# A scheduled attention and expert kernel: elementwise work moved from GpSimd to VectorE, new planner rules, a third buffer

## The chip, the cores and the metric

The kernel runs on one core of a Trainium2 chip. The metric is the device time of one execution in microseconds (us). The kernel before took 844.2 us, the median of 3 runs (843.67 to 844.75).

## The reference

Three stages follow one another, in float32 (2 batches, 8 heads, 576 positions, head size 64; so 1152 tokens of 512):

```python
# 1 attention, with the 32 largest scores of each row kept
scores = scale * np.matmul(q, k.transpose(0, 1, 3, 2))
kth = np.partition(scores, -32, axis=-1)[..., -32:-31]
attn = softmax(np.where(scores >= kth, scores, -1e9))   # written out
x = (attn @ v), heads side by side                      # 1152 x 512
# 2 four experts, all of them for every token
for e in range(4):                                      # w1[e] 512 x 1024, w2[e] 1024 x 512
    y += p[:, e:e+1] * (np.maximum(x @ w1[e], 0.0) @ w2[e])
# 3 a gated layer                                       # w_a, w_b 512 x 1536, w_out 1536 x 512
return (y @ w_a) * (y @ w_b) @ w_out
```

The three weights of stage 3 come in as 64-bit floats, and the kernel makes float32 of them itself.

## The kernel before

**Work.** The 1152 tokens are nine tiles of 128, in four groups of 1, 2, 3 and 3 tiles. While one group is in the top-32 search of stage 1 (VectorE, L772 and L780), TensorE works on the experts of the groups before it. Matrices are multiplied in a reduced float format, so each operand is split into a high part (a copy on ScalarE) and a low part (operand minus high part), and a product is three matmuls (high x high, high x low, low x high). L492 is the line of every matmul, L495 that of every transpose.

Per expert and group: ScalarE evicts relu(x w1) as the high part (L1007), VectorE makes the low part (L1011); both free the PSUM bank and feed the second matmul. L1036 adds the results to y. The weights' own parts are L937 (ScalarE) and L938 (GpSimd for the early groups, VectorE for the late ones).

Stage 3 computes y w_a and y w_b together by Strassen's scheme, with seven products of half size in place of eight. It needs sums of y's parts first. `combine` makes them, once for group 2 (with all groups before it) and once for group 3 (`own`). For each half: four `whole` sums of a high and a low part (L1085), the differences s1, s3, s2, s4 (L1108 to L1111; s1 of group 3 is L1105), a high part (L1112) and its low part (L1113), and three of each at once (L1115, L1116). In group 2 all but the high parts run on GpSimd. In group 3 the differences run on VectorE and the four sums on GpSimd; L1095 to L1103 evict the transposed y. `multiply` then evicts a first product with ScalarE (L1328), adds the other six to it on VectorE (L1319), multiplies the two results on GpSimd (L1322, twice), and splits the outcome into a high part (L1339, ScalarE) and a low part (L1340, GpSimd). There are 24 such calls: six steps, two units each, two sets of columns (320 and 256 wide). The second matmul adds up over the steps in SBUF (L1361, L1364).

The weights of stage 3 are prepared in the background: `double` makes a float32 from a 64-bit one with three VectorE instructions (the first L1224, the last L1227), two on ScalarE and an integer addition on GpSimd (L1230); `narrow` and `d_unit` make sums and parts of these (L1246, L1247, L1266 to L1273).

**Buffers.** The intermediate sums of `combine` and `multiply` lie in slots named tp, of which there are two, in the region `low`. A slot is free when its last reader is done.

**Order.** Nothing of this is ordered by hand. Each call registers an `Op` with its engine, a cost, a key (a smaller one goes first), what it waits for and the slots it uses. `Plan.order` simulates all engines, and at each step gives a free engine the ready Op of the smallest key. It does so 42 times with random delays added; from the seventh time on the early part is kept from the best order so far, up to one of the times in `STAGES` (50 to 400 us). `rerun` then goes through each order three times with delays, and the one with the smallest mean end is emitted. Each engine's instructions run in that order on the chip and wait for semaphores only. An Op with `port=True` (VectorE instructions that work in SBUF alone) isn't started in the simulation while GpSimd is busy:

```python
ok = not (op.port and free.get("POOL", 0.0) > now)
```

Of the kernel before, what the change touches and what calls it, by code (L numbers as in the profile page):

```python
# [84 lines left out]
class Op:  # L85
    __slots__ = ("engine", "hold", "lag", "key", "emit", "waits", "after", "tiles", "n", "start", "left", "at", "nbytes", "port", "late", "since")

SEEN, SEEN_PE = 45, 130  # L90
COLD, COLD_END = 1.7, 46e3
ISSUE, LAND, GBS, LANES = 500, 2100, 320.0, 8

STAGES = 0.0, 50e3, 110e3, 170e3, 230e3, 300e3, 400e3
ORDERS, RERUNS, SHAKE, LATE_ENGINE, LATE_DMA, LOG = 42, 3, 25.0, 40.0, 800.0, False


class Plan:  # L100
# [37 lines left out]
    def rerun(self, got, draw):  # L138

        free, end, dma, users = {}, {}, 0.0, {}  # L140
        last = 0.0
        for op in got:
# [10 lines left out]
            if op.engine == "SP":  # L153
                free["SP"] = t + ISSUE
                dma = max(dma, t + ISSUE) + op.nbytes / GBS
                e = dma + LAND + draw.uniform(0.0, LATE_DMA)
            else:
                free[op.engine] = t + hold
                e = t + hold + op.lag + (draw.uniform(0.0, LATE_ENGINE) if op.engine != "PE" else 0.0)
# [8 lines left out]
    def order(self):  # L168
# [28 lines left out]
        dma_free, lanes = 0.0, []  # L197
        queue, now, done = [(op.since, -1, None) for op in self.ops if op.since], 0.0, []
        heapq.heapify(queue)
        seq = 0  # L200
# [25 lines left out]
        def pick(engine):  # L226
# [6 lines left out]
            while ready_:  # L233
                item = heapq.heappop(ready_)
                op = item[2]

                ok = not (op.port and free.get("POOL", 0.0) > now)
                for t in op.tiles:
                    if t.slot is None and (t.slots in stuck or place(t) is None):
                        if t.n == t.slots.next:  # L240
                            stuck.add(t.slots)
                        ok = False
                if ok:
                    found = op
# [8 lines left out]
        while len(done) < len(self.ops):  # L253
            moved = False
            for engine in free:
# [20 lines left out]
                else:  # L276
                    hold = op.hold * COLD if engine == "PE" and now < COLD_END else op.hold
                    free[engine] = now + hold
                    end = now + hold + op.lag + op.late
                heapq.heappush(queue, (end, op.n, op))  # L280
                heapq.heappush(queue, (free[engine], -1, None))
# [5 lines left out]
            while queue and queue[0][0] <= now:  # L287
# [3 lines left out]
                if isinstance(op, Buffer):  # L291
                    op.slots.free.add(op.slot)
                    continue
                for t in op.tiles:
# [18 lines left out]
def dve(n):  # L313
    return 62 + 1.04 * n
# [18 lines left out]
FILL = 9  # L333
SLACK = 1200

# [5 lines left out]
def body(tc, q, k, v, probs, w1, w2, wa, wb, wo, out):  # L341
# [61 lines left out]
    xf = const("xf", [128, KD, 128])  # L403
    vrem = [const(f"vrem{b}", [128, H, D]) for b in range(B)]
    qrem = const("qrem", [128, H, D])
    kscr = dr.tile([B, HP, 2 * D, 2, S], F32, name="kscr")
# [45 lines left out]
    vvs = low.slots("vv", 2, 2048)  # L452
    tps = low.slots("tp", 2, 4 * 320)
    mid.again()
# [597 lines left out]
    def combine(c, y, yd):  # L1052
# [9 lines left out]
        x0, x1 = slice(c0, c0 + n), slice(c1, c1 + n)  # L1062
        K = -1500 if own else -1000
        got = []
# [12 lines left out]
        def pair_(w, emit, after, tiles, sbuf=True):  # L1077
            if own:
                return vector(dve(w), lambda: emit(nc.vector), K, after, tiles, port=sbuf)
            return gpsimd(pool_(w), lambda: emit(nc.gpsimd), K, after, tiles)  # L1080

        def whole(out, k, cols, tp):
            w = cols.stop - cols.start
            return gpsimd(
                pool_(w), lambda: nc.gpsimd.tensor_tensor(out(), xs[:, 0, k, cols], xs[:, 1, k, cols], op=ALU.add), K,  # L1085
                sum((ydone[g, k] for g in range(len(GROUPS) - 1)), []), [tp]
            )
# [127 lines left out]
    def double(src, s, t, ts, n):  # L1215
# [14 lines left out]
        return gpsimd(pool_(512), lambda: nc.gpsimd.tensor_tensor(  # L1230
            t().bitcast(I32), fold(c.ap.bitcast(I32)), fold(lowv().bitcast(I32)), op=ALU.add), s, [o4, o5], [c, d, ts])

# [44 lines left out]
    def gated():  # L1277
# [32 lines left out]
        def multiply(un, own, g):  # L1310

            m = sets[own][2]
            tp = tps.tile()
            tv = lambda i, j=None: tp.ap[:, i * m:(j or i + 1) * m]
# [6 lines left out]
            def mul(out, i, j, after):  # L1321
# [103 lines left out]
```

## Time and profile before

| | |
|---|---|
| median of 3 runs | 844.2 us |
| profiled execution | 842.55 us, of it the span 840.8 us |
| TensorE busy | 800.8 us, 95% of the span |
| VectorE busy | 730.9 us, 87% |
| ScalarE busy | 535.1 us, 64% |
| GpSimd busy | 420.8 us, 50% |

All times come from one execution, and the shares are means over stages of different kinds. PE is TensorE, PEld its weight loads, DVE VectorE, ACT ScalarE, POOL GpSimd, SP the queue that issues transfers. L12 is line 12 of the kernel before. "Idle before" at an instruction or a group is the time in which its engine stood still just before it, with what ended that. Matmuls are pipelined, so their own durations overlap.

### The profile page before, as it was taken

The page shows a single profiled execution, that of the slowest core. Times are in us where ns is not written, and L with a number is a line of the kernel's source. Part 1 is how long each engine was busy: PE and PEld are TensorE (multiplying, and loading weights), DVE is VectorE, ACT ScalarE, POOL GpSimd, SP SyncE. Part 2 cuts the span into 40 slices and gives each one's busy share as a digit, 9 for nine tenths or more (in the row PEclk, how much of TensorE's full clock was granted, in tenths as well). Part 3 has the DMA queues.
Part 4 walks back from the last instruction along what each step waited for, and adds up shares of the span by engine and source line. Part 5 has one row for each costly group of instructions (what it writes and reads, how often), then busy time and mean ns, then how long its engine had stood idle before and what let it go on. Part 6 is the DMA issues. An engine that isn't in the chain of part 4 may idle for free.

```text
span 840.8 us, 14615 instructions
## 1 busy us (share of the span) xinstructions
PE 800.8 (95%) x5285; PEld 710.7 (85%) x5285; DVE 730.9 (87%) x1399; ACT 535.1 (64%) x953; POOL 420.8 (50%) x381
## 2 busy tenths in 40 slices
PE   7689999999999999999999998999999999999997
PEld 6577777798888889999899887888988889799996
DVE  7999999999899999999977967889858898986654
ACT  6879887998898989897756647666424532331210
POOL 3524433888977966854221393222226465372432
PEclk8699999999999999999999999999999999999999
DMA  6849977765455443523246637987311223211013
GB/s 218 249 132 318 326 214 215 228 182 180 154 189 155 132 151 102 169 76 126 76 128 195 190 114 274 318 281 249 104 50 51 101 79 100 73 51 50 2 51 112
DMA packets 91416, 129.68 MB, mean 154 GB/s; under 512 B 10832, under 2 KB 67152, under 8 KB 89808
## 3 DMA queue, kind: packets, MB, share of 16 engines
q1 hardware_dynamic: 91344, 128.75, 47.7%
q8 instruction: 41, 0.67, 0.3%
q14 instruction: 31, 0.25, 0.1%
HBM read 115.36 MB, written 13.37 MB: 153 GB/s over the span
## 4 chain that ended last, share of the span: by engine, by line
PE 52%; DVE 25%; ACT 8%; POOL 8%; issue 4%; DMA 2%; POOLq 0%; SPq 0%; DVEq 0%; ACTq 0%
PE ps L492 50%; DVE low L772 10%; DVE low L780 8%; PE ps L495 2%; POOL mid L938 2%; ACT low L803 1%; ACT mid L937 1%; POOL low L1085 1%; ACT low L811 1%; POOL low L1230 1%; DVE big L1273 1%; ACT lowa L751 1%; DVE low L1036 1%; POOL low L807 1%; DVE mid L1011 1%
## 5 line engine op out<-in xcount | busy, mean ns | idle before, releaser
L492 PE MATMUL ps<-mid 128*128 128x512 f32 x1092 | 279.5, 397 | 6.6 <-ACT mid L1007 3.2
L492 PEld LDWEIGHTS ps<-mid 128*128 128x128 f32 x1092 | 199.5, 189 | 45.0 <-ACT mid L1007 3.8
L492 PE MATMUL ps<-xs,mid 128*128 128x384 f32 (+1 forms) x1152 | 203.7, 321 | 3.5 <-DVE mid L1011 3.3
L492 PEld LDWEIGHTS ps<-xs,mid 128*128 128x128 f32 x1152 | 184.3, 189 | 13.1 <-DVE mid L1011 5.1
L772 DVE MAX8 low<-low 128x8 f32<-128x576 f32 x216 | 154.9, 747 | 0.1
L938 POOL TENSOR_TENSOR mid<-raw,mid 128x1024 fp32r<-128x1024 f32 x48 | 114.9, 2407 | 8.8 <-ACT mid L937 6.2
L807 POOL TENSOR_TENSOR low<-lowa,low 128x576 f32<-128x576 f32 x70 | 98.9, 1431 | 34.4 <-ACT low L803 28.1
L1230 POOL TENSOR_TENSOR low<-low 128x512 int32<-128x512 int32 x36 | 54.0, 1499 | 116.7 <-DVE low L1227 86.7
L937 ACT ACTIVATE mid<-raw 128x1024 fp32r<-128x1024 f32 x96 | 101.8, 1071 | 10.8 <-PE ps L492 9.4
L780 DVE MATCH_REPLACE8 low<-low 128x576 f32<-128x576 f32 x144 | 106.2, 743 | 0.0
L1319 DVE TENSOR_TENSOR low<-ps,low 128x320 f32<-128x320 f32 (+1 forms) x168 | 72.1, 452 | 27.0 <-PE ps L492 25.7
L1322 POOL TENSOR_TENSOR low<-low 128x320 f32<-128x320 f32 (+1 forms) x48 | 46.4, 968 | 91.6 <-DVE low L1319 82.0
L492 PE MATMUL ps<-xs,big 128*128 128x320 f32 (+1 forms) x576 | 87.5, 297 | 3.0 <-ACT low L1328 2.5
L492 PEld LDWEIGHTS ps<-xs,big 128*128 128x128 f32 x576 | 80.8, 190 | 6.2 <-ACT low L1328 2.8
L938 DVE TENSOR_TENSOR mid<-raw,mid 128x1024 fp32r<-128x1024 f32 x48 | 65.4, 1362 | 8.9 <-ACT mid L937 8.5
L1007 ACT ACTIVATE mid<-ps 128x384 fp32r<-128x384 f32 (+1 forms) x96 | 44.3, 465 | 38.2 <-PE ps L492 35.0
L492 PE MATMUL ps<-lowa_again,big 128*128 128x320 f32 (+1 forms) x432 | 66.9, 297 | 0.0
L1011 DVE SCALAR_TENSOR_TENSOR mid<-ps,mid 128x384 fp32r<-128x384 f32 (+1 forms) x96 | 47.9, 504 | 17.6 <-ACT mid L1007 17.4
L492 PEld LDWEIGHTS ps<-lowa_again,big 128*128 128x128 f32 x432 | 61.0, 190 | 2.4 <-DVE low L1319 0.6
L822 ACT ACTIVATE low<-low 128x576 f32<-128x576 f32 x70 | 51.5, 785 | 16.9 <-DVE low L819 16.8
L495 PE MATMUL ps<-identr,low 128*128 128x128 f32 x360 | 51.7, 279 | 9.8 <-ACT low L822 8.9
L803 ACT ACTIVATE low<-lowa,low 128x576 f32<-128x576 f32 x70 | 53.6, 782 | 11.6 <-POOL low L797 11.4
(119 smaller groups left out, 1240.7 us busy)
## 6 DMA issues: line engine op xcount, KB each, us to landing
raw<-in_moe_w_dram SPq DMA_DIRECT2D x122, 512.0 KB, 3.9
big<-kscr SPq DMA_DIRECT2D x20, 576.0 KB, 5.1
low<-in_v_dram SPq DMA_DIRECT2D x24, 256.0 KB, 3.5
low<-in_moe_w_b_dram SPq DMA_DIRECT2D x12, 512.0 KB, 3.6
low<-in_moe_w_a_dram SPq DMA_DIRECT2D x12, 512.0 KB, 4.3
low<-in_moe_w_out_dram SPq DMA_DIRECT2D x12, 512.0 KB, 4.2
wscr<-big SPq DMA_DIRECT2D x6, 1024.0 KB, 6.1
mid<-wscr SPq DMA_DIRECT2D x6, 1024.0 KB, 4.8
```

The lines of the kernel that those rows point to most:

```text
L492: nc.tensor.matmul(out, l, r, **kw)
L495: nc.tensor.transpose(out, a, i)
L772: 62 + 1.04 * width, lambda at=at, cs=cs: nc.vector.max(m8v()[:, x, cs], at()), key + 0.02 * r, [done],
L780: lambda at=at, cs=cs: nc.vector.match_replace(out=src[1](), in_to_replace=m8v()[:, x, cs], in_values=at(), imm_value=LOW),
L803: S, lambda x=x, s=s: nc.scalar.activation(ev(x), s.ap, AF.Relu, bias=endv()[:, x, 1:2], scale=-STEEP),
L807: pool_(S), lambda x=x, s=s: nc.gpsimd.tensor_tensor(ev(x), s.ap, ev(x), op=ALU.subtract), ks, [a], [s, ep]
L822: S, lambda x=x: nc.scalar.activation(ev(x), ev(x), AF.Copy, scale=sums.ap[:, x:x + 1]),
L937: hi = scalar(1024, lambda: nc.scalar.activation(u.ap[:, 0:1024], r.ap, AF.Copy), 500 + s, [ld], [u, r], sbuf=True)
L938: sub = lambda eng: eng.tensor_tensor(u.ap[:, 1024:2048], r.ap, u.ap[:, 0:1024], op=ALU.subtract)
L1011: lambda h=h, p=p: nc.vector.scalar_tensor_tensor(h.ap[:, n:2 * n], p.ap[:, 0:n], 0.0, h.ap[:, 0:n], op0=ALU.max, op1=ALU.subtract),
L1230: return gpsimd(pool_(512), lambda: nc.gpsimd.tensor_tensor(t().bitcast(I32), fold(c.ap.bitcast(I32)), fold(lowv().bitcast(I32)), op=ALU.a ...
L1319: return vector(dve(m), lambda: nc.vector.tensor_tensor(tv(out), p.ap[:, 0:m], tv(i), op=ALU.add), K, [o] + after, [p, tp])
```

## The change

Six things change. (1) The planner treats all GpSimd Ops as port Ops too, and starts neither engine's port Op while the other engine runs one. (2) Where two meet in a rerun, each goes on at a fixed share of its speed. (3) The sums and differences of `combine` for group 2 and the sums for group 3 go to VectorE, and those of group 2 get the key 1190 in place of -1000: behind all expert work (-100 and 500 on), just ahead of the weights of stage 3 (1210 on). (4) The low part in `multiply` (L1340) goes to VectorE. (5) A third tp slot lies in the memory of what is kept of v's and q's last rows, which attention reads; every third request takes it. (6) The planner reckons 600 ns more until the result of `double` is seen (`EASE`).

```diff
+OTHER = {"DVE": "POOL", "POOL": "DVE"}
+RATES = {"DVE": 0.65, "POOL": 0.5}
+def contend(engine, hold, other, left):
+    a, b = RATES[engine], RATES[other]
+    t = min(hold / a, left / b)
+    return t + hold - a * t, t + left - b * t
...
+BLOCK = True
@@ rerun, and the same in order, with the Op met pushed back to its later end
+                if op.port:
+                    other = OTHER[op.engine]
+                    y = runs.get(other)
+                    if y is not None and free[other] > t:
+                        hold, left = contend(op.engine, hold, other, free[other] - t)
+                        end[id(y)] += t + left - free[other]
+                        free[other] = t + left
@@ order, pick
-                ok = not (op.port and free.get("POOL", 0.0) > now)
+                y = runs.get(OTHER[engine]) if BLOCK and op.port else None
+                ok = y is None or free[y.engine] <= now
@@ body
-SLACK = 1200
+SLACK, EASE = 1200, 600
-    vrem = [const(f"vrem{b}", [128, H, D]) for b in range(B)]
-    qrem = const("qrem", [128, H, D])
+    rest = Region("rest", 3 * H * D, F32)
+    vrem = [rest.t[:, i * H * D:(i + 1) * H * D].rearrange("p (h d) -> p h d", d=D) for i in range(B + 1)]
+    qrem = vrem.pop()
-    tps = low.slots("tp", 2, 4 * 320)
+    tps = [low.slots("tp", 2, 4 * 320), rest.slots("tpr", 1, 4 * 320)]
+    def sums_slot():
+        taken_.append(0)
+        return tps[len(taken_) % 3 == 0].tile()
-    def gpsimd(hold, emit, key, after, tiles):
-        return plan.add("POOL", hold, emit, key, after, tiles, lag=55)
+    def gpsimd(hold, emit, key, after, tiles, lag=55):
+        return plan.add("POOL", hold, emit, key, after, tiles, lag=lag, port=True)
@@ combine
-        K = -1500 if own else -1000
+        K = -1500 if own else 1190
@@ pair_
-            if own:
-                return vector(dve(w), lambda: emit(nc.vector), K, after, tiles, port=sbuf)
-            return gpsimd(pool_(w), lambda: emit(nc.gpsimd), K, after, tiles)
+            return vector(dve(w), lambda: emit(nc.vector), K, after, tiles, port=sbuf)
@@ whole
-            return gpsimd(
-                pool_(w), lambda: nc.gpsimd.tensor_tensor(out(), xs[:, 0, k, cols], xs[:, 1, k, cols], op=ALU.add), K,
+            return vector(
+                dve(w), lambda: nc.vector.tensor_tensor(out(), xs[:, 0, k, cols], xs[:, 1, k, cols], op=ALU.add), K,
@@ half, multiply
-            tp = tps.tile()
+            tp = sums_slot()
@@ multiply
-            lo = gpsimd(pool_(2 * m), lambda: nc.gpsimd.tensor_tensor(
-                g.ap[:, n:2 * n][:, cs], tv(0, 2), g.ap[:, 0:n][:, cs], op=ALU.subtract), K, [hi], [g, tp])
+            lo = vector(dve(2 * m), lambda: nc.vector.tensor_tensor(
+                g.ap[:, n:2 * n][:, cs], tv(0, 2), g.ap[:, 0:n][:, cs], op=ALU.subtract), K, [hi], [g, tp], port=True)
```

What the new plan makes of it shows in the order of the instructions. The lines of the changed kernel have other numbers: L1126 there is L1085 here, L1149 to L1152 are L1108 to L1111, L1153, L1154, L1156 and L1157 are L1112, L1113, L1115 and L1116, L1050 and L1054 are L1007 and L1011, L980 and L981 are L937 and L938, L1137, L1144 and L1146 are L1096, L1103 and L1105, and L1369, L1360, L1363 and L1381 are L1328, L1319, L1322 and L1340.

GpSimd of the kernel before, where it makes the sums for group 2 (L1230 is the addition of `double`):

```order
L1230 TENSOR_TENSOR low<-low 128x512
L1085 TENSOR_TENSOR low<-xs 128x320 x4
L1108 TENSOR_TENSOR low<-low 128x320
L1109 TENSOR_TENSOR low<-low 128x320
L1113 TENSOR_TENSOR xs<-low,xs 128x320
L1110 TENSOR_TENSOR low<-low 128x320
L1111 TENSOR_TENSOR low<-low 128x320
L1116 TENSOR_TENSOR lowa_again<-low,lowa_again 128x3x320
L1085 TENSOR_TENSOR low<-xs 128x320 x4
```

The second half follows in the same way. In the changed kernel GpSimd has nothing at this place but the additions of `double`; the sums stand on VectorE, the first half as follows (L1265 to L1268 are `double`):

```order
L1126 TENSOR_TENSOR low<-xs 128x320 x3
L1054 SCALAR_TENSOR_TENSOR mid<-ps,mid 128x384 x2
L1126 TENSOR_TENSOR low<-xs 128x320
L1265 TENSOR_SCALAR low<-low 128x512
L981 TENSOR_TENSOR mid<-raw,mid 128x1024
L1149 TENSOR_TENSOR low<-low 128x320
L1266 TENSOR_SCALAR low<-low 128x512
L1150 TENSOR_TENSOR low<-low 128x320
L1154 TENSOR_TENSOR xs<-low,xs 128x320
L1151 TENSOR_TENSOR low<-low 128x320
L1268 SCALAR_TENSOR_TENSOR low<-low 128x512
L1152 TENSOR_TENSOR low<-low 128x320
```

So they are spread among expert work and weights. ScalarE at the same place, before:

```order
L1007 ACTIVATE mid<-ps 128x384
L1112 ACTIVATE xs<-low 128x320
L1007 ACTIVATE mid<-ps 128x384
L937 ACTIVATE mid<-raw 128x1024
L1115 ACTIVATE lowa_again<-low 128x3x320
L1007 ACTIVATE mid<-ps 128x384
```

and ScalarE in the changed kernel:

```order
L1153 ACTIVATE xs<-low 128x320
L1050 ACTIVATE mid<-ps 128x384
L980 ACTIVATE mid<-raw 128x1024
L1050 ACTIVATE mid<-ps 128x384
L1156 ACTIVATE lowa_again<-low 128x3x320
L1050 ACTIVATE mid<-ps 128x384
```

The copy that waits for the last difference (L1115, now L1156) stands one eviction of an expert later. On VectorE that difference follows that eviction's low part in the changed kernel:

```order
L1151 TENSOR_TENSOR low<-low 128x320
L981 TENSOR_TENSOR mid<-raw,mid 128x1024
L1054 SCALAR_TENSOR_TENSOR mid<-ps,mid 128x384
L1152 TENSOR_TENSOR low<-low 128x320
L1266 TENSOR_SCALAR low<-low 128x512
```

So the second difference of the pair now waits for an expert's eviction between the two. VectorE where the sums for group 3 are made, before:

```order
L1096 TENSOR_TENSOR xs<-ps,xs 128x128
L1105 TENSOR_TENSOR low<-ps,low 128x256
L1103 TENSOR_TENSOR xs<-ps,xs 128x384
L1109 TENSOR_TENSOR low<-low 128x256
L1110 TENSOR_TENSOR low<-low 128x256
L1113 TENSOR_TENSOR xs<-low,xs 128x256
L1111 TENSOR_TENSOR low<-low 128x256
L1105 TENSOR_TENSOR low<-ps,low 128x256
L1109 TENSOR_TENSOR low<-low 128x256
L1110 TENSOR_TENSOR low<-low 128x256
L1116 TENSOR_TENSOR lowa_again<-low,lowa_again 128x3x256
```

and in the changed kernel, from the same instruction to the first L1157 (L1381 is the low part of a product, in the slot of the new region `rest`):

```order
L1137 TENSOR_TENSOR xs<-ps,xs 128x128
L1152 TENSOR_TENSOR low<-low 128x256
L1126 TENSOR_TENSOR low<-xs 128x128
L1144 TENSOR_TENSOR xs<-ps,xs 128x384
L1146 TENSOR_TENSOR low<-ps,low 128x256
L1381 TENSOR_TENSOR mid<-rest,mid 128x640
L1157 TENSOR_TENSOR lowa_again<-low,lowa_again 128x3x256
L1150 TENSOR_TENSOR low<-low 128x256
L1154 TENSOR_TENSOR xs<-low,xs 128x256
L1151 TENSOR_TENSOR low<-low 128x256
L1360 TENSOR_TENSOR rest<-ps,rest 128x320
```

Ahead of these rows stand L1137, L1146, L1126, L1144, L1150, L1154 and L1151, each once, behind the seven additions of the product before. The low part now stands on VectorE, ahead of L1157, and the additions of the next product follow. Two of the four sums of group 3 (L1126, 128 columns) are made long before, behind those of group 2; the other two stand here.

## Rows read from the trace of the kernel before

**Rows 1.** Busy time by stage: stretch, length, PE, PEld, DVE, ACT, POOL, clock, DMA, GB/s.
```profile
302.00:480.00 178.00, 177.58 (x1236) 161.94 (x1235) 165.09 (x312) 138.10 (x249) 74.88 (x67) 1.00 0.40 128
480.00:520.00 40.00, 36.35 (x172) 31.53 (x171) 26.29 (x31) 20.63 (x33) 29.90 (x24) 0.96 0.55 172
520.00:600.00 80.00, 78.49 (x393) 70.30 (x392) 71.59 (x104) 50.06 (x76) 21.29 (x14) 1.00 0.80 267
600.00:632.00 32.00, 29.84 (x176) 27.86 (x174) 21.37 (x39) 10.71 (x24) 5.79 (x8) 1.00 0.17 53
632.00:756.00 124.00, 121.21 (x765) 110.25 (x766) 107.00 (x198) 49.13 (x79) 72.67 (x58) 1.00 0.24 77
756.00:836.00 80.00, 80.00 (x491) 73.40 (x489) 46.55 (x85) 11.09 (x19) 26.63 (x26) 1.00 0.14 49
836.00:841.00 5.00, 0.03 (x1) 0.00 (x0) 0.69 (x1) 0.00 (x0) 0.00 (x0) 0.81 0.43 127
```
**Rows 2.** TensorE's waits from 302 us on: for whom, us in total, times, longest.
```profile
PE ps L492 <- ACT mid L1007: 3.2, 2, 2.5
PE ps L492 <- ACT low L1328: 2.5, 1, 2.5
PE ps L492 <- DVE mid L1011: 2.0, 2, 1.5
PE ps L492 <- DVE raw L1364: 1.4, 3, 0.5
```
**Rows 3.** The chain that ended last, 478 to 510 us: start, us, what.
```profile
480.80 4.33 POOL low L1085 x4
...
494.45 5.23 POOL low L1085 x4
```
**Rows 4.** Instructions in order of time near 506 us: start, us, what [idle before].
```profile
505.52 1.00 ACT L1115 ACTIVATE lowa_again<-low 128x960 fp32r<-128x960 f32 x1 [3.07 <-POOL low L1111]
...
506.96 5.43 PE L492 MATMUL ps<-mid 128*128 128x512 f32 x15 [2.54 <-ACT mid L1007]
```
**Rows 5.** The same view, 623 to 633 us.
```profile
623.91 0.29 DVE L1096 TENSOR_TENSOR xs<-ps,xs 128x128 fp32r<-128x128 f32 x1
...
626.47 1.66 POOL L1340 TENSOR_TENSOR mid<-low,mid 128x640 fp32r<-128x640 f32 x1 [0.84 <-ACT mid L1339]
626.72 1.68 DVE L1110 TENSOR_TENSOR low<-low 128x256 f32<-128x256 f32 x1
...
631.89 0.44 ACT L1328 ACTIVATE low<-ps 128x320 f32<-128x320 f32 x1 [1.10 <-DVE lowa_again L1116]
...
632.38 1.15 PE L492 MATMUL ps<-xs,big 128*128 128x320 f32 x6 [2.54 <-ACT low L1328]
```
**Rows 6.** The same view, 584 to 590 us.
```profile
584.72 2.06 POOL L1230 TENSOR_TENSOR low<-low 128x512 int32<-128x512 int32 x1 [9.86 <-DVE low L1227]
585.55 1.52 DVE L1224 TENSOR_SCALAR low<-low 128x512 f32<-128x512 f32 x1
...
588.78 1.49 PE L492 MATMUL ps<-xs,mid 128*128 128x384 f32 x7 [1.51 <-DVE mid L1011]
```
**Rows 7.** GpSimd by shape, 302 us on: count, busy us, mean ns, idle before.
```profile
L1340 POOL TENSOR_TENSOR mid<-low,mid 128x640 fp32r<-128x640 f32 x12 | 19.0, 1587 | 10.7 <-ACT mid L1339 10.7
L1340 POOL TENSOR_TENSOR mid<-low,mid 128x512 fp32r<-128x512 f32 x12 | 16.7, 1389 | 9.7 <-ACT mid L1339 9.7
```
**Rows 8.** VectorE in the same view.
```profile
L1247 DVE TENSOR_TENSOR big<-low,big 128x512 fp32r<-128x512 f32 x12 | 9.3, 779 | 3.8 <-ACT big L1246 3.8
...
L1116 DVE TENSOR_TENSOR lowa_again<-low,lowa_again 128x768 fp32r<-128x768 f32 x2 | 1.9, 948 | 0.0
...
L1109 DVE TENSOR_TENSOR low<-low 128x256 f32<-128x256 f32 x2 | 0.8, 420 | 0.1
...
L1096 DVE TENSOR_TENSOR xs<-ps,xs 128x128 fp32r<-128x128 f32 x2 | 0.6, 286 | 0.1
```
**Rows 9.** GpSimd's busy time on L1340 alone in one stretch: us (count), clock, DMA.
```profile
632.00:756.00 124.00, 21.09 (x14) 1.00 0.24 77
```

More of the change, by code (lines that the diff above doesn't have):

```diff
@@ L85 @@
 class Op:
-    __slots__ = ("engine", "hold", "lag", "key", "emit", "waits", "after", "tiles", "n", "start", "left", "at", "nbytes", "port", "late", "since")
+    __slots__ = ("engine", "hold", "lag", "key", "emit", "waits", "after", "tiles", "n", "start", "left", "at", "nbytes", "port", "late", "since", "fin")
 SEEN, SEEN_PE = 45, 130
 COLD, COLD_END = 1.7, 46e3
+OTHER = {"DVE": "POOL", "POOL": "DVE"}
[4 more added lines that the diff above has]
+    return t + hold - a * t, t + left - b * t
 ISSUE, LAND, GBS, LANES = 500, 2100, 320.0, 8
 STAGES = 0.0, 50e3, 110e3, 170e3, 230e3, 300e3, 400e3
+BLOCK = True
 ORDERS, RERUNS, SHAKE, LATE_ENGINE, LATE_DMA, LOG = 42, 3, 25.0, 40.0, 800.0, False
@@ L140, in rerun @@
         free, end, dma, users = {}, {}, 0.0, {}
-        last = 0.0
+        last, runs = 0.0, {}
         for op in got:
@@ L157, in rerun @@
             else:
+                if op.port:
[5 more added lines that the diff above has]
+                        free[other] = t + left
+                if op.engine in OTHER:
+                    runs[op.engine] = op if op.port else None
                 free[op.engine] = t + hold
@@ L198, in order @@
         queue, now, done = [(op.since, -1, None) for op in self.ops if op.since], 0.0, []
+        runs = {}
         heapq.heapify(queue)
@@ L277, in order @@
                     hold = op.hold * COLD if engine == "PE" and now < COLD_END else op.hold
+                    if op.port:
+                        other = OTHER[engine]
+                        y = runs.get(other)
+                        if y is not None and free[other] > now:
+                            hold, left = contend(engine, hold, other, free[other] - now)
+                            y.fin += now + left - free[other]
+                            free[other] = now + left
+                            heapq.heappush(queue, (y.fin, y.n, y))
+                            heapq.heappush(queue, (free[other], -1, None))
+                    if engine in OTHER:
+                        runs[engine] = op if op.port else None
                     free[engine] = now + hold
                     end = now + hold + op.lag + op.late
+                op.fin = end
                 heapq.heappush(queue, (end, op.n, op))
@@ L292, in order @@
                     op.slots.free.add(op.slot)
+                    continue
+                if op.fin > now:
                     continue
@@ L452, in body @@
     vvs = low.slots("vv", 2, 2048)
-    tps = low.slots("tp", 2, 4 * 320)
+    tps = [low.slots("tp", 2, 4 * 320), rest.slots("tpr", 1, 4 * 320)]
+    taken_ = []
+    def sums_slot():
+        taken_.append(0)
+        return tps[len(taken_) % 3 == 0].tile()
     mid.again()
@@ L1077, in pair_ @@
         def pair_(w, emit, after, tiles, sbuf=True):
-            if own:
-                return vector(dve(w), lambda: emit(nc.vector), K, after, tiles, port=sbuf)
-            return gpsimd(pool_(w), lambda: emit(nc.gpsimd), K, after, tiles)
+            return vector(dve(w), lambda: emit(nc.vector), K, after, tiles, port=sbuf)
         def whole(out, k, cols, tp):
             w = cols.stop - cols.start
-            return gpsimd(
-                pool_(w), lambda: nc.gpsimd.tensor_tensor(out(), xs[:, 0, k, cols], xs[:, 1, k, cols], op=ALU.add), K,
-                sum((ydone[g, k] for g in range(len(GROUPS) - 1)), []), [tp]
+            return vector(
+                dve(w), lambda: nc.vector.tensor_tensor(out(), xs[:, 0, k, cols], xs[:, 1, k, cols], op=ALU.add), K,
+                sum((ydone[g, k] for g in range(len(GROUPS) - 1)), []), [tp], port=True
             )
         def half(a):
-            tp = tps.tile()
+            tp = sums_slot()
             tv = lambda i, j=None: tp.ap[:, i * n:(j or i + 1) * n]
@@ L1230, in double @@
         return gpsimd(pool_(512), lambda: nc.gpsimd.tensor_tensor(
-            t().bitcast(I32), fold(c.ap.bitcast(I32)), fold(lowv().bitcast(I32)), op=ALU.add), s, [o4, o5], [c, d, ts])
+            t().bitcast(I32), fold(c.ap.bitcast(I32)), fold(lowv().bitcast(I32)), op=ALU.add), s, [o4, o5], [c, d, ts], EASE)
     def narrow(f):
@@ L1312, in multiply @@
             m = sets[own][2]
-            tp = tps.tile()
+            tp = sums_slot()
             tv = lambda i, j=None: tp.ap[:, i * m:(j or i + 1) * m]
```

## The prediction, made before the changed kernel ran

> **What bounds the kernel now.** I read first the busy time by stage, with the bounds of the stages put where the kind of work changes [rows 1]. In each row the first number after the length is TensorE's busy time. From 302 to 480 us it is busy 177.58 of 178, and from 756 to 836 it never stops: there TensorE is the bound and nothing that other engines do better can show. What is left lies between: it is idle 40 - 36.35 = 3.65 us in 480:520, 1.51 in 520:600, 2.16 in 600:632 and 2.79 in 632:756. With 0.42 in 302:480 that is 10.5 us. In 480:520 the granted clock is 0.96 as well, so for some 3.2 us of those 40 TensorE ran at its lower level, 1.2 GHz, and did 1.6 us less work. Behind its last matmul the kernel still needs 4.97 us (836:841) for the last eviction and the store. So the ceiling of what this change can win behind 302 us is 10.5 + 1.6 = 12.1 us.
>
> Then I asked who ends TensorE's waits there [rows 2]: L1007, L1328 and L1011 have the long ones, each of them an eviction that stands in a queue behind something else. The rest of the reading is to find that something.
>
> The longest is at 507 us. The chain of work runs almost over GpSimd alone from 481 to 505 us; its largest pieces are the sums of x (L1085, twice four of them in 4.33 and 5.23 us) [rows 3], with the differences behind them. ScalarE's copy L1115 waits 3.07 us for GpSimd's L1111, and TensorE waits 2.54 us for L1007 [rows 4], which only stands behind that copy in ScalarE's queue. The drop of the clock follows on that idle time.
>
> The second is at 632 us [rows 5]: TensorE waits 2.54 us for L1328, and that one for a slot that L1116 frees. In the same rows VectorE's L1110 takes 1.68 us, against the 420 ns of a like one (L1109) [rows 8], because GpSimd's L1340 had begun just before it and holds on for 1.66 us.
>
> The third is at 588.8 us [rows 6]: GpSimd's L1230 and VectorE's L1224 collide in the same manner, L1224 takes 1.52 us, and L1011, queued behind it, lets TensorE wait 1.51 us.
>
> **Part 1, the order.** The planner's new rules put no instruction on the chip. Up to 302 us every engine's order is the old one (the first 474 VectorE, 440 ScalarE, 177 GpSimd instructions that the program issues, and 167 of SyncE's transfers), so I price that stretch at nothing. In 302:480 the order differs in detail, but TensorE is idle only 0.42 us there: at best -0.4, and since VectorE is busy 165.09 of 178, +1 at worst; I take 0. The DMA order behind that follows the same plan; no wait of TensorE in [rows 2] ends on a transfer, so I cost it at 0 too.
>
> **Part 2, the sums of x for group 2.** Twenty instructions leave GpSimd, which was busy 29.9 us in 480:520 [rows 1], and join VectorE. On VectorE a 256-wide one takes 0.420 us and a 768-wide one 0.948 [rows 8], about 1.03 ns a column more. So 320 columns are 0.486 us and 960 are 1.146, and the two halves cost 2 x (9 x 0.486 + 1.146) = 11.0 us. VectorE is busy 26.29 of the 40 us from 480 to 520, so this fits in its idle time: 37.3 of 40 if all of it fell there. Their priority now lies behind all expert work, and their results are only needed by the products, more than 100 us later. What goes is ScalarE's 3.07 us. What is late next shows in the orders above: the second copy of that kind (L1156 of the changed kernel) stands one expert eviction behind the one that its last difference waits for on VectorE. That is about an L1011 and a 320-wide difference, some 1.1 us of ScalarE's wait instead of 3.07, and by the same offset as now (3.07 against 2.54) 0.6 us of TensorE's. So 2.6 of the 3.65 us go, and with the gap short I take the clock to stay up: 2.6 + 1.6 = 4.2 us. Bounds: all 5.25, or nothing if VectorE's fuller queue holds L1011 back instead.
>
> **Part 3, the third slot and the four sums of group 3.** L1328 now writes the third slot, so it no longer waits for L1116 but for the low part of the product before, L1340, which is L1381 in the changed kernel and stands 12 instructions behind L1137 on VectorE (L1096 before). Those rows are two of 128 from PSUM and two sums (4 x 0.286), two L1146 and four of L1150 to L1154 (6 x 0.42), two L1144 of 384 columns (0.55 each) and the low part (0.82): 5.6 us. Before, L1328 started 631.89 - 623.91 = 7.98 us behind the same row [rows 5]. That is 2.4 us earlier; I take 1.9 for the gaps between instructions. Bounds: 0, if the slot is free but VectorE's queue is as late, and 2.54.
>
> **Part 4, the low parts.** 24 instructions leave GpSimd (19.0 + 16.7 = 35.7 us [rows 7]) for VectorE. By the rows used above 640 columns cost 0.816 and 512 cost 0.684 us: 18.0 us; by L1247, which does the same on 512 columns among collisions (779 ns), 21.0 us [rows 8]. I take 19, or 0.79 each. 14 of them stand in 632:756 [rows 9], where VectorE is busy 107.0 of 124 us [rows 1]; it becomes 107.0 + 14 x 0.79 = 118.1, or 95%. The cover is thin there. A low part also waits for ScalarE's copy L1339: on GpSimd these waits were 10.7 + 9.7 us [rows 7]. Behind the waiting one on VectorE now stand the additions L1360, which free the PSUM banks that TensorE needs. The plan puts other rows between, so I take 0, and a rival below has the rest. In return GpSimd has 21.09 us less in that stretch, and collisions like those of [rows 5, 6] go with it; I count none of that.
>
> The collisions bear on how the plan is made, too. In [rows 6] GpSimd's L1230 needs 2.06 us, and L1224 ends 0.29 us behind it, though it was issued while L1230 ran: one waits for the other as a whole. The Trainium skill (SBUF — State Buffer, Who interferes with whom) says just that: the port pair of VectorE and GpSimd is an exclusive lock, whoever comes second is blocked until the first is done. The trace agrees. The changed planner prices an overlap as a share (0.65 and 0.5 of the speed) in the runs by which it chooses among its orders. By the share L1110 of [rows 5] would have cost 0.42/0.65 = 0.65 us, by the lock the 1.68 of its row. This makes the second rival below, whose time is worked out from rows.
>
> **Sum.** 4.2 + 1.9 = 6.1 us off; the wait at 588.8 us and the rest I leave as they are. The profiled execution has a span of 840.8 and a time of 842.55, so it should come to 834.7 and 836.4. The median of the runs is 844.2, 1.65 above the profiled one: 838.1.
>
> **Rivals.**
> - All waits go: nothing but TensorE's own work is left behind 302 us. For it: each large wait hangs on a GpSimd instruction that moves or gets thinner. Against: the 1.4 us on L1364 come in three waits of at most 0.5 [rows 2], behind TensorE's own sums. 844.2 - 12.1 = 832.1.
> - The plan does not do what it says. Its order keeps the two engines apart only if the chip keeps to the plan's times, and its choice rests on a price that [rows 6] contradicts. Then waits as long as the ones removed come back at other places, as at 588.8 us: 844.2. Against it: the two gains above come from moved work and from a slot, not from the choice.
> - VectorE becomes the bound in 632:756, which is slower. It is idle 17 us there, of which the low parts take 11.1. If it cannot be filled beyond its 86% of now, because it waits for L1339 with the additions queued behind, the stretch lasts 118.1 / 0.863 = 136.8 us, 12.8 more: 844.2 - 6.1 + 12.8 = 850.9. It decides from 5.9 us of such waits on, since 118.1 + 5.9 = 124; GpSimd's waits of 20.4 us over all 24 say that it can happen, the rows between in the order speak against it.
>
> **Chances.** Forecast 0.64 (its own range 834.5 to 841.5), all waits gone 0.12, waits come back 0.13, VectorE bound 0.11. About 0.2%, 1.7 us, is what a measurement of this kernel can tell from no change. Faster takes the first two and 0.03 of the third: 0.79. Of the third 0.08 lies within 0.2% and 0.02 above; slower is 0.13. The range leaves out the far end of the first rival and most of the last: 833 to 846.
>
> **What would show it.** In the profile after, TensorE's waits for L1007's successor at about 500 us should be under 1 us with the granted clock at 1.00 over 480:520, the one for L1328's at about 630 us under 1 us, GpSimd's busy time lower by about 60 us and VectorE's higher by 25 to 32. Wrong would be the forecast if TensorE's idle time in 632:756 rose from 2.79 us above 6, with VectorE as the one that ends it, or if a wait of over 2 us stood anywhere between 302 and 632 us.

## The result: 828.7 us, 1.8% faster, and the profile after

The changed kernel takes 828.74 us, the median of 4 runs (827.81 to 829.76), against 843.93 for the kernel before in 4 runs. The ratio is 0.982, with a 95% interval of 0.9803 to 0.9837. So 15.2 us went, where 6.1 were forecast; the direction was right, the time lies outside the range. The profiled execution took 828.9 us, with a span of 827.1 us.

The same view by stage as [rows 1], its bounds moved with the work:

```profile
302.00:480.00 178.00, 177.66 (x1236) 161.94 (x1235) 163.21 (x309) 139.40 (x248) 73.40 (x67) 1.00 0.40 130
480.00:520.00 40.00, 40.00 (x209) 36.65 (x208) 37.27 (x63) 25.21 (x40) 6.08 (x4) 1.00 0.57 191
520.00:600.00 80.00, 80.00 (x407) 72.86 (x406) 70.07 (x103) 49.49 (x74) 19.55 (x14) 1.00 0.76 257
600.00:630.00 30.00, 29.05 (x181) 26.83 (x180) 22.59 (x50) 10.65 (x23) 4.37 (x5) 1.00 0.17 61
630.00:745.00 115.00, 114.67 (x737) 106.68 (x736) 102.55 (x197) 48.46 (x78) 43.31 (x40) 1.00 0.25 83
745.00:822.00 77.00, 77.00 (x476) 70.88 (x474) 51.45 (x98) 9.81 (x17) 16.17 (x18) 1.00 0.13 49
822.00:827.00 5.00, 0.38 (x2) 0.00 (x0) 0.69 (x1) 0.00 (x0) 0.00 (x0) 0.80 0.50 153
```

From 302 us to the last matmul TensorE is idle for 1.6 us in all, and its granted clock is 1.00 in every stretch up to there. VectorE is busy 37.27 of 40 us in 480:520, GpSimd 6.08. TensorE's waits, as in [rows 2]:

```profile
PE ps L535 <- ACT rest L1369: 0.8, 1, 0.8
PE ps L535 <- DVE low L1079: 0.3, 1, 0.3
PE ps L535 <- DVE low L1360: 0.2, 1, 0.2
```

The waits of [rows 4, 6] have no successor. That of [rows 5] is 0.8 us long, for L1369, whose slot the low part L1381 now frees, as foreseen:

```profile
621.04 0.82 DVE L1381 TENSOR_TENSOR mid<-rest,mid 128x640 fp32r<-128x640 f32 x1
621.77 0.95 DVE L1157 TENSOR_TENSOR lowa_again<-low,lowa_again 128x768 fp32r<-128x768 f32 x1
621.95 0.44 ACT L1369 ACTIVATE rest<-ps 128x320 f32<-128x320 f32 x1 [0.37 <-DVE mid L1381]
...
622.44 1.14 PE L535 MATMUL ps<-lowa_again,big 128*128 128x320 f32 x6 [0.84 <-ACT rest L1369]
```

TensorE's idle time tells too little of where the 15 us went. The view of groups gives a 512-column matmul a mean of 394 ns, while in a run of them the next one begins after about 230 ns:

```profile
L535 PE MATMUL ps<-mid 128*128 128x512 f32 x1092 | 278.7, 394 | 1.4 <-POOL mid L981 1.3
```

```profile
503.71 4.96 PE L535 MATMUL ps<-mid 128*128 128x512 f32 x21
```

A stop of up to some 0.16 us between two of them therefore shows as no idle time, and a longer one shows shorter by that. So I also took every matmul's start from the trace, summed what its distance to the next is beyond the median distance of its shape (rows and columns) in the kernel before, and cut the sum at equal amounts of matmul work. The columns are the places where the cuts fall in the kernel before, in us; a minus is work at shorter distances than the median. The runs below the second row are explained in the next section.

| us lost, by equal work | to 303 | to 485 | to 541 | to 618 | to 673 | to 752 | to the end |
|---|---|---|---|---|---|---|---|
| before | 58.1 | 3.5 | 5.8 | 2.2 | 5.0 | 3.6 | 0.3 |
| changed kernel | 59.6 | 2.5 | 0.1 | 0.0 | 1.9 | 0.7 | 0.0 |
| old_order_vector | 60.2 | 3.3 | 0.3 | 2.4 | 3.1 | 8.1 | 1.7 |
| all_but_rules | 60.0 | 3.4 | 0.1 | 0.1 | 3.2 | 6.4 | 0.0 |
| slot_only | 59.1 | 2.9 | 7.1 | 0.4 | 4.0 | 3.8 | 0.3 |
| apart_only | 58.8 | 2.5 | 0.1 | 0.2 | 4.4 | 0.1 | -0.2 |
| apart_slot | 59.0 | 3.0 | 0.1 | 0.2 | 1.3 | -0.1 | -0.1 |
| nothing_apart | 58.7 | 3.4 | 12.7 | 3.7 | 10.3 | 6.2 | 0.1 |
| slower_prices | 113.7 | 3.1 | 0.2 | 0.0 | 5.4 | 0.1 | 1.1 |
| one_swap | 59.1 | 3.6 | 5.2 | 2.3 | 5.9 | 4.2 | 0.3 |

By this measure the changed kernel wins 15.2 us behind the first cut (20.4 us lost before, 5.2 now). Ahead of that, with the same order, its profiled execution lost 1.5 us more than the one of before; the medians don't show that.

### The profile page after: what moved, and what is told of

Its sections match the earlier page's. It is cut to its first block, busy times and chain, and to the rows that moved or that the text cites. A ratio compares the mean times of both kernels' runs of the same rounds, so it can differ in the third digit from the quotient of the medians.

```text
span 827.1 us, 14615 instructions
## 1 busy us (share of the span) xinstructions
PE 795.7 (96%) x5285; PEld 711.2 (86%) x5285; DVE 738.8 (89%) x1447; ACT 537.4 (65%) x953; POOL 351.7 (43%) x333
## 4 chain that ended last, share of the span: by engine, by line
PE 65%; DVE 17%; ACT 10%; POOL 3%; issue 3%; DMA 1%; SPq 0%; POOLq 0%; DVEq 0%; ACTq 0%
PE ps L535 63%; DVE low L815 8%; DVE low L823 6%; PE ps L538 3%; POOL mid L981 2%; ACT mid L980 2%; ACT low L854 1%; ACT low L846 1%; ACT lowa L794 1%; ACT low L865 1%; ACT lowa L923 1%; DMA raw<-in_moe_w_dram 1%; POOL low L850 1%; ACT mid L1050 1%; DVE mid L1054 0%
## 5 line engine op out<-in xcount | busy, mean ns | idle before, releaser
L1271 POOL TENSOR_TENSOR low<-low 128x512 int32<-128x512 int32 x36 | 51.3, 1424 | 169.7 <-DVE low L1268 110.4
L981 POOL TENSOR_TENSOR mid<-raw,mid 128x1024 fp32r<-128x1024 f32 x48 | 115.0, 2409 | 7.4 <-ACT mid L980 5.5
L980 ACT ACTIVATE mid<-raw 128x1024 fp32r<-128x1024 f32 x96 | 102.1, 1072 | 16.6 <-PE ps L535 12.0
L981 DVE TENSOR_TENSOR mid<-raw,mid 128x1024 fp32r<-128x1024 f32 x48 | 63.1, 1314 | 6.7 <-ACT mid L980 6.6
L1050 ACT ACTIVATE mid<-ps 128x384 fp32r<-128x384 f32 (+1 forms) x96 | 44.3, 464 | 35.2 <-PE ps L535 32.5
L1054 DVE SCALAR_TENSOR_TENSOR mid<-ps,mid 128x384 fp32r<-128x384 f32 (+1 forms) x96 | 48.3, 505 | 12.7 <-ACT mid L1050 12.3
L538 PEld LDWEIGHTS ps<-identr,low 128*128 128x128 f32 x360 | 42.7, 144 | 17.8 <-ACT low L865 11.3
L794 ACT ACTIVATE lowa<-ps 128x576 f32<-128x576 f32 x72 | 47.4, 663 | 15.4 <-POOL low L850 11.3
```

Source lines behind the costliest of these rows:

```text
L538: nc.tensor.transpose(out, a, i)
L794: S, lambda: nc.scalar.activation(s.ap.rearrange("p (c n) -> p c n", c=2), at.ap[:, :, 0:HALF], AF.Copy),
L980: hi = scalar(1024, lambda: nc.scalar.activation(u.ap[:, 0:1024], r.ap, AF.Copy), 500 + s, [ld], [u, r], sbuf=True)
L981: sub = lambda eng: eng.tensor_tensor(u.ap[:, 1024:2048], r.ap, u.ap[:, 0:1024], op=ALU.subtract)
L1050: n, lambda h=h, p=p: nc.scalar.activation(h.ap[:, 0:n], p.ap[:, 0:n], AF.Relu), -1000, [o], [h, p]
L1271: return gpsimd(pool_(512), lambda: nc.gpsimd.tensor_tensor(t().bitcast(I32), fold(c.ap.bitcast(I32)), fold(lowv().bitcast(I32)), op=ALU.a ...
```

## Experiments

First the question was whether the place of the work (theory A) or the order (theory B) makes the gain. Then which part of the change makes the order, and at last how the order saves time. Where no other is named, times are medians of 4 or more runs, and each ratio is to runs of the kernel before on the same chip.

| run | us | ratio, 95% interval |
|---|---|---|
| lo_on_gpsimd | 828.86 | 0.9813 (0.9792 to 0.9834) |
| sums_on_gpsimd | 832.0 | 0.9852 (0.9831 to 0.9873) |
| both_on_gpsimd | 831.55 | 0.9852 (0.9826 to 0.9878) |
| old_order_vector | 843.14 | 0.998 (0.9968 to 0.9991) |
| rules_only | 830.96 | 0.9846 (0.983 to 0.9863) |
| all_but_rules | 837.09 | 0.9922 (0.9907 to 0.9937) |
| two_slots | 832.5 | 0.9866 (0.9851 to 0.9881) |
| slot_only | 840.26 | 0.9959 (0.9945 to 0.9973) |
| ease_only | 840.13 | 0.9953 (0.9937 to 0.997) |
| apart_only | 830.08 | 0.9835 (0.982 to 0.985) |
| draws_after | 827.76 | 0.9808 (0.9793 to 0.9822) |
| draws_before | 841.8 | 0.9972 (0.996 to 0.9984) |
| apart_slot | 828.33 | 0.9804 (0.9774 to 0.9834) |
| nothing_apart | 858.99 | 1.0168 (1.0137 to 1.0199) |
| slower_prices | 888.01 | 1.0516 (1.0477 to 1.0555) |
| lock_price | 828.85 | 0.9814 (0.9781 to 0.9846) |
| one_swap | 844.76 | 1.0005 (0.9993 to 1.0018) |
| more_orders | 826.89 | 0.9793 (0.977 to 0.9816) |

**The place of the work, in a fixed order.** In the changed kernel the work is planned for VectorE, and only the issuing engine is another:

```diff
 # lo_on_gpsimd; sums_on_gpsimd does the same in pair_ (group 2) and whole
-            lo = vector(dve(2 * m), lambda: nc.vector.tensor_tensor(
+            lo = vector(dve(2 * m), lambda: nc.gpsimd.tensor_tensor(
```

> The changed kernel with every engine's order as it is, but the 24 low parts (L1381) are issued on GpSimd again, at the same place of the order. If the place where the work runs made the gain (theory A): the small waits of the stretch 630 to 745 us come back, 4 to 5 us, so 833 to 834 us. If the order that the new planner rules found made it (theory B): GpSimd has idle time there, under 1.5 us, so 829 to 830 us.

> The changed kernel's order, with the 20 sums and differences of group 2 and the four sums of group 3 issued on GpSimd again. Theory A: ScalarE's copies wait for GpSimd near 500 us as before, 4 to 6 us, so 833 to 835 us. Theory B: the lower priority has spread them and given ScalarE other work ahead, under 1.5 us, so 829 to 830 us.

> Both of these at once, so that order and third slot alone are left of the change. Theory A: 8 us or more of the 15 are lost, 837 to 842 us. Theory B: 829 to 832 us.

The low parts are worth nothing: 828.86. GpSimd has its 24 us more in the stretch, and TensorE doesn't stop:

```profile
630.00:745.00 115.00, 115.00 (x740) 107.08 (x740) 97.40 (x183) 48.93 (x78) 67.70 (x55) 1.00 0.27 83
```

The sums cost 3 us when they are put back alone or with the low parts: less than theory A said (833 us or more), more than B did (829 to 830). For both at once A expected the loss of 8 us or more; B holds for most of the gain.

The opposite, the old order with the 48 instructions on VectorE:

```diff
-            lo = gpsimd(pool_(2 * m), lambda: nc.gpsimd.tensor_tensor(
+            lo = gpsimd(pool_(2 * m), lambda: nc.vector.tensor_tensor(
 # and in pair_ and whole alike
```

> The kernel before with its own order and its two slots, but the 48 instructions (sums of x for both groups, low parts) are issued on VectorE at the same places of the order. Theory A: 5 to 9 us of the 15 are won, 835 to 839 us. Theory B: the order was made for GpSimd and VectorE's queue now holds its evictions back: 842 to 847 us.

It wins 0.2%. The wait near 507 us is gone (0.3 in the table above, to 541 us), and 4.5 us come back in the gated stage, where VectorE's queue was ordered for other work:

```profile
PE ps L492 <- DVE low L1319: 4.1, 7, 0.8
PE ps L492 <- DVE raw L1364: 2.0, 2, 1.0
PE ps L492 <- DVE mid L1011: 2.0, 2, 1.5
PE ps L492 <- ACT low L1328: 1.9, 1, 1.9
```

**The parts, planned anew.** rules_only is the kernel before with the new rules and nothing else. all_but_rules is the changed kernel with the old ones. two_slots and slot_only differ by the third slot:

```diff
 # all_but_rules
-                y = runs.get(OTHER[engine]) if BLOCK and op.port else None
-                ok = y is None or free[y.engine] <= now
+                ok = not (engine == "DVE" and op.port and free.get("POOL", 0.0) > now)
-SLACK, EASE = 1200, 600
+SLACK, EASE = 1200, 55
 # and no price of an overlap
 # two_slots
-        return tps[len(taken_) % 3 == 0].tile()
+        return tps[0].tile()
```

> The kernel before with the planner's new rules alone (the two engines kept apart, the price of an overlap, EASE of 600 ns); no work moves, two slots, the old priority. It is planned anew. If the rules found the better order (theory B1): two thirds of the 15 us or more, 829 to 834 us. If the third slot made it possible (B2): 840 to 845 us, since TensorE's waits in the gated stage stay. If any new draw of the planner's delays would do as much (B3): anything from 832 to 846 us.

> The changed kernel planned by the old rules (only VectorE's SBUF work waits for GpSimd in the plan, no price of an overlap, EASE back at 55 ns); moved work, priority 1190 and third slot stay. B1: most of the gain is lost, 838 to 845 us. B2: under 3 us are lost, 829 to 832 us. B3: anything from 829 to 842 us.

> The changed kernel, planned anew with the two old slots alone. B1: under 3 us are lost, 829 to 832 us. B2: L1369 waits for a slot again near 630 us and the small waits of 630 to 745 us come back, 6 to 9 us lost, 835 to 838 us. B3: anything from 829 to 838 us.

> The kernel before with the third slot alone, planned anew by the old rules. B1: only the wait of 2.5 us near 630 us goes, 841 to 843 us. B2: that wait and the ones of the gated stage go, 6 to 9 us, 835 to 838 us. B3: anything from 835 to 846 us.

The rules alone win 13 of the 15 us, with the moved work back on GpSimd. One long wait is left, and it is the slot's:

```profile
PE ps L534 <- ACT low L1370: 2.8, 1, 2.8
PE ps L534 <- DVE low L1078: 0.3, 1, 0.3
PE ps L534 <- DVE xs L1187: 0.2, 1, 0.2
```

Without the rules 8 us are lost, most of them in the gated stage (6.4 us lost to 752 in the table above, 0.7 in the changed kernel); the waits near 507 and 588.8 us go there too, by the moved work and the new plan. The slot is worth 3.8 us in the changed kernel (two_slots). The 3.7 us of slot_only are less clear: at the slot's place, 618 to 673, its profiled execution wins 1.0. B2 is wrong for the gated stage: its small waits don't need the slot to go. all_but_rules lies between the ranges of B1 and B2; two_slots and slot_only lie within 1 us outside those of B1.

**Which rule, and whether it was luck.**

```diff
 # ease_only, on the kernel before: double's addition
+            ..., [c, d, ts], 600)
 # apart_only, on the kernel before: the rule ok = ... of the change, port=True for GpSimd; EASE 55, no price
 # draws_after, draws_before
-            draw = random.Random(r)
+            draw = random.Random(r + 1000)
```

> The kernel before, planned anew, with one number changed: the result of double's addition on GpSimd counts as seen 600 ns later. If this reserve is what the rules' gain rests on (C1): 830 to 835 us. If it is that the plan keeps the two engines apart (C2): 840 to 845 us. If it is the price of an overlap by which the best of 42 orders is chosen (C3): 840 to 845 us. If a lucky draw (C4): anything from 832 to 846.

> The kernel before, planned anew, with one rule more: GpSimd's instructions too wait in the plan until VectorE's SBUF work is done. No price of an overlap, no reserve. C1: 840 to 845 us. C2: 830 to 835 us. C3: 838 to 845 us. C4: anything from 832 to 846.

> The changed kernel with other random delays in the 42 draws of the planner; nothing else. Under C1 to C3 the order comes out as good, within 2 us of 828.7. Under C4 it can lose 5 us or more.

> The kernel before with other random delays in the 42 draws; nothing else. Under C1 to C3 it stays within 3 us of 844. Under C4 it can win 5 us or more, to 830 to 839 us.

apart_only has 13.6 us of the gain: one condition in the planner. The reserve alone wins 3.6 us. One other set of draws moves either kernel by 1 to 2 us, and of all kernels planned anew here those with the rule took 826.9 to 832.5 us, those without it 837.1 or more. So luck is not the cause, but differences of 1 to 2 us between kernels planned anew say little.

**What the condition gives the plan.** apart_slot is apart_only with the third slot. nothing_apart drops the old half of the rule as well. slower_prices keeps the old rule and makes the plan's times a quarter longer. lock_price changes the price of an overlap in the changed kernel:

```diff
 # nothing_apart, on the kernel before
-                ok = not (op.port and free.get("POOL", 0.0) > now)
+                ok = True
 # slower_prices, on the kernel before
-        return plan.add("POOL", hold, emit, key, after, tiles, lag=55)
+        return plan.add("POOL", hold * 1.25, emit, key, after, tiles, lag=55)
 # and hold * 1.25 for VectorE's port Ops
 # lock_price, on the changed kernel, in contend
-    t = min(hold / a, left / b)
-    return t + hold - a * t, t + left - b * t
+    return left + hold, left
```

> The kernel before, planned anew, with the one rule that GpSimd's instructions too wait in the plan for VectorE's SBUF work, and with the third slot; no work moves, no priority, no reserve, no price. If rule and slot are the whole gain and the moved work is worth nothing: 827 to 829 us. If the moved work is worth what it cost when it was put back in the changed kernel's order (3 us): 831 to 833 us.

> The kernel before, planned anew, without its old half of the rule: in the plan neither engine waits for the other. If the plan must count the time in which the two shut each other out (theory D1): worse than before, 848 to 856 us. If it is only the new half, GpSimd behind VectorE, that matters (D2): within 3 us of 844.

> The kernel before, planned anew by the old rule, with all GpSimd work and VectorE's SBUF work priced a quarter longer in the plan. If the plan's times only have to be long enough on average, as the chip's are (D3): two thirds of the gain, 831 to 836 us. If it has to know which instructions shut each other out, and when (D1): under a third of it, 840 to 846 us.

> The changed kernel with the overlap in the reruns priced as the profile shows it: the one that comes second waits until the first is done. If the choice among the 42 orders by this price matters (C3): 1 to 3 us faster, 826 to 828 us. If the blocked plan has already decided it: within 1.5 us of 828.7.

Rule and slot are the whole gain: 828.33 with no work moved. Neither engine waiting in the plan costs 15 us (3 more than D1 said), one waiting is the kernel before, both waiting wins 13.6. lock_price decides nothing, and its trace shows why: every engine runs the instructions of the changed kernel in the same order, so the other price chose the same order.

slower_prices, at 888.01, lies outside both of its ranges, and doesn't refute D3. All its loss lies ahead of the first cut (113.7 us in the table above, against 58.1). Behind it, 10.0 us are lost, where the kernel before loses 20.4 and apart_only 7.2, though hardly less work is left there (769 VectorE instructions, against 762):

```profile
480.00:600.00 120.00, 120.00 (x680) 108.86 (x679) 91.90 (x127) 69.79 (x106) 43.33 (x35) 1.00 0.50 155
600.00:800.00 200.00, 196.68 (x1181) 182.85 (x1180) 166.06 (x297) 93.81 (x155) 90.48 (x75) 0.99 0.41 140
```

So behind 302 us a plan by the old rule with longer times wins 10.4 us, where apart_only wins 13.2. Whether the plan must know that the engines shut each other out, or only has to reckon enough time, stays open; that its first part came late may have helped, too.

Is it that the two engines meet less on the chip? By the groups' means, no. First the kernel before, then rules_only, from 302 us on:

```profile
L938 DVE TENSOR_TENSOR mid<-raw,mid 128x1024 fp32r<-128x1024 f32 x48 | 65.4, 1362 | 8.9 <-ACT mid L937 8.5
L1230 POOL TENSOR_TENSOR low<-low 128x512 int32<-128x512 int32 x36 | 54.0, 1499 | 116.7 <-DVE low L1227 86.7 <-ACT mid L1007 26.8 <-ACT low L1229 2.8
```

```profile
L980 DVE TENSOR_TENSOR mid<-raw,mid 128x1024 fp32r<-128x1024 f32 x48 | 64.9, 1352 | 11.8 <-ACT mid L979 11.5
L1272 POOL TENSOR_TENSOR low<-low 128x512 int32<-128x512 int32 x36 | 54.2, 1506 | 122.3 <-DVE low L1269 74.8 <-ACT mid L1049 22.0 <-issue 8.4
```

These two take as long as ever (1362 and 1352 ns, 1499 and 1506). I also summed, over all VectorE and GpSimd instructions behind the first cut, what each takes beyond a fast one of its shape (the 5th percentile over the runs here): 62 us before, 64 in rules_only, 58 in apart_only, 76 in nothing_apart. So rules_only wins its 13 us without fewer meetings; in nothing_apart more of them come with the loss. The order is what differs. In apart_slot GpSimd makes the same sums at the same place as before, and is as late with them. But ScalarE's copy for them (L1152 there) stands behind the eviction (L1044), not ahead of it as in [rows 4], and neither it nor TensorE waits:

```profile
503.62 5.64 PE L529 MATMUL ps<-mid 128*128 128x512 f32 x24
503.81 0.49 ACT L1044 ACTIVATE mid<-ps 128x384 fp32r<-128x384 f32 x1 [2.54 <-PE ps L529]
...
505.29 1.01 ACT L1152 ACTIVATE lowa_again<-low 128x960 fp32r<-128x960 f32 x1
```

**One exchange by hand.** If so, the same exchange in the kernel before should give its wait back. The last run tries more orders, for a version faster than both:

```diff
 # one_swap, on the kernel before, behind plan.best(): the copy (h2) and what hangs on it (l2);
 # evict holds ScalarE's relu evictions (L1007)
+    nxt_ = min((o for o in evict if at[id(o)] > at[id(h2)]), key=lambda o: at[id(o)])
+    moved = [o for o in (h2, l2) if at[id(o)] < at[id(nxt_)]]
+    got = [o for o in got if o not in moved]
+    i = got.index(nxt_) + 1
+    got[i:i] = moved
 # more_orders, on apart_slot
-ORDERS = 42
+ORDERS = 126
```

> The kernel before in its own order, with one exchange: on ScalarE the second copy that waits for GpSimd's sums (L1115 before, L1117 here) is issued behind the next L1007 instead of ahead of it. Everything else stands as it stood. If the order in ScalarE's queue is what cost the wait near 507 us: 3 to 5.5 us faster, 838.5 to 841 us, and the clock does not fall there. If GpSimd's long chain itself is the cost: within 1 us of before.

> Rule and third slot alone as in apart_slot, with 126 orders tried in place of 42, as an attempt at a version faster than both. From 302 us on TensorE hardly waits any more, so what is left is in the first 302 us, which VectorE's search holds: 825 to 828.5 us.

The exchange wins nothing: 844.76. In the trace ScalarE's queue differs by this one exchange and no other engine's order does. The time is the one that I gave for GpSimd's long chain as the cost, but the trace shows something else. The wait of 2.54 us did go: it is 0.40 and 0.68 us there, and the clock stays up. But 14 us later a new one of 1.89 us stands, where TensorE had none: VectorE's L938, which meets GpSimd's addition, takes 2.16 us with the low part L1012 queued behind it.

```profile
517.82 1.31 POOL L1233 TENSOR_TENSOR low<-low 128x512 int32<-128x512 int32 x1 [2.58 <-DVE low L1230]
...
518.05 2.16 DVE L938 TENSOR_TENSOR mid<-raw,mid 128x1024 fp32r<-128x1024 f32 x1 [0.46 <-ACT mid L937]
...
520.73 2.87 PE L492 MATMUL ps<-xs,mid 128*128 128x384 f32 x15 [1.89 <-DVE mid L1012]
```

In the kernel before the same two meet at this place, and L938 takes as long. There TensorE, later by its long wait, still has matmuls to run, and doesn't notice:

```profile
515.51 7.52 PE L492 MATMUL ps<-xs,mid 128*128 128x384 f32 x42
...
517.21 1.32 POOL L1230 TENSOR_TENSOR low<-low 128x512 int32<-128x512 int32 x1 [4.13 <-DVE low L1227]
...
517.46 2.16 DVE L938 TENSOR_TENSOR mid<-raw,mid 128x1024 fp32r<-128x1024 f32 x1 [0.47 <-ACT mid L937]
```

More waits follow (5.9 and 4.2 in the table, where before has 5.0 and 3.6). My expectation was wrong: the long wait had covered a later one. Mending one place isn't enough; here the time went only where the whole order was made anew. more_orders is the fastest run, 826.89 (825.52 to 828.22); with apart_slot at 828.33 it is within what other draws do.

## Why the prediction was wrong, point by point

- **What bounds the kernel** was read right: behind 302 us TensorE, with waits in between that could go, and almost all of them went. The ceiling of 12.1 us was too low, since idle time hides short stops: by the matmuls' starts 15.2 us went.
- **Part 1, the order, is the step that failed.** It said that the new rules put no instruction on the chip, and priced the order behind 302 us at 0. The rule that keeps the engines apart is worth 13.6 us by itself (apart_only). I had the orders before me and priced single exchanges in them, at two places, for the moved work; the order as a whole was no term of the sum. The rest of the sum nearly holds without the rules: all_but_rules, the change planned by the old ones, wins 6.8 us where 6.1 were forecast. That is in part luck, since two terms put at nothing cancel: the waits near 588.8 us went (2.1), and the gated stage lost 2.8 more. What the new condition adds, GpSimd waiting for VectorE, stood at [rows 6]. The prediction read 2.06 us as what GpSimd's L1230 needs there; it needs 1.30 at 588.49 us, and at 584.72 it came while VectorE's L938 ran (the lines are in the last section). I set this aside and weighed the price of an overlap instead, which decides nothing (lock_price, 828.85 against 828.74).
- **Part 2, the sums:** 4.2 us were forecast; in that stretch 5.7 went, but the rule alone does it (0.1 left in apart_only) with the sums still on GpSimd. The move does it too, without the rule (0.1 in all_but_rules, 0.3 in old_order_vector): the mechanism was right, and the move is one of two ways. Nothing is won by it that rule and slot don't win too. That VectorE's busy time in 480:520 came out as worked out, 37.27 us against 37.3, is partly luck: 63 instructions ran there, 32 more than before, where 20 were reckoned. In the whole profile VectorE is busy 7.9 us more (738.8 against 730.9), not 25 to 32, and GpSimd 69 us less, where about 60 were said.
- **Part 3, the slot:** 1.9 us forecast, 3.8 measured by taking it away, 1.7 between the medians of apart_only and apart_slot and 3.1 between their profiles at the slot's place (618 to 673). The mechanism is right.
- **Part 4, the low parts:** taken as free, and they are (lo_on_gpsimd). VectorE is busy 89% in 630:745, less than the 95% worked out.
- **The wait at 588.8 us** was left as it is; it went with the order. So did the small waits of the gated stage, 2.9 us between 673 and 752.
- **Rivals.** The nearest was that all waits go, given 0.12. That the plan doesn't do what it says is refuted. A busy VectorE held nothing up in the new order; it did in the orders made without the rules (8.1 us lost to 752 in old_order_vector, 6.4 in all_but_rules, 3.6 before), which is where that rival was right.

What exactly the plan of before had wrong at each place isn't shown; that its order fails where an instruction is late by a meeting is shown at [rows 5, 6] and in one_swap. Nor is it shown whether the new rule helps by its knowledge of the lock or by the time that it reserves.

## What to carry to other kernels

Where a planner orders the queues, one rule in its model can be worth more than the work that is moved (here 13.6 us against none): look in the trace for what the model leaves out (two engines that shut each other out), and price the whole order, not the two places where it is seen to change. A single long wait is no estimate of what its removal brings, since it can cover later ones. Busy work on an engine with slack can be moved or left, if the order is made for it.

## What the runs showed of the hardware

In these traces a VectorE instruction that works in SBUF and one of GpSimd hold each other up, whichever comes second. In one_swap VectorE's L938 began 0.23 us behind GpSimd's addition of 1.31 us; it took 2.16 us and ended 1.08 us behind the addition, where one that met nothing takes 1.21. The other way round, an L938 that came 0.16 us ahead of the addition took 1.22 us, and the addition 2.23:

```profile
510.65 1.21 DVE L938 TENSOR_TENSOR mid<-raw,mid 128x1024 fp32r<-128x1024 f32 x1
...
512.84 1.22 DVE L938 TENSOR_TENSOR mid<-raw,mid 128x1024 fp32r<-128x1024 f32 x1
513.00 2.23 POOL L1233 TENSOR_TENSOR low<-low 128x512 int32<-128x512 int32 x1 [2.82 <-DVE low L1230]
```

The kernel before has it near [rows 6]: the same addition, L1230 there, takes 2.06 us behind an L938, and 1.30 the next time:

```profile
584.41 1.22 DVE L938 TENSOR_TENSOR mid<-raw,mid 128x1024 fp32r<-128x1024 f32 x1
584.72 2.06 POOL L1230 TENSOR_TENSOR low<-low 128x512 int32<-128x512 int32 x1 [9.86 <-DVE low L1227]
...
588.49 1.30 POOL L1230 TENSOR_TENSOR low<-low 128x512 int32<-128x512 int32 x1 [1.70 <-DVE low L1227]
```

A short instruction can so take several times its own duration: L1110 in [rows 5], 1.68 us against 0.42.

And the first 302 us of the same order differ by up to 2.2 us from one profiled execution to another (58.1 to 60.3 us lost by the same measure in the sixteen kernels whose order is the same up to there), as much as other draws are worth.
